# A fused attention and gated-MLP kernel: warm-up operands, weight loads, one input load and one logits group moved

## The chip, the core and the metric

One core of a Trainium2 chip runs the whole program: TensorE (PE, matmuls into PSUM), VectorE (DVE), ScalarE (ACT), GpSimd (POOL), and SyncE (SP), which here only issues DMAs. The metric is the device time of one execution in microseconds (us), the median of several runs. Inputs and output lie in DRAM. A profile of one execution gives the times of single instructions.

## The reference

Two branches read the same layer-normalised x (2048 rows of 640, bfloat16) and are added to x:

```python
x = A_x
xn = _layernorm(x, axis=-1)
return x + _A_ref(xn, A_wqkv, A_wo) + _B_ref(xn, B_w_gate, B_w_up, B_w_down)

def _A_ref(x, wqkv, wo):
    H = 32; Dh = D // H                    # 32 heads of 20
    W, dil = 8, 2                          # each row looks at itself and 7 rows before it, 2 apart
    qkv = ...                              # x @ wqkv, split into q, k, v per head
    idx = pos[:, None] - off[None, :]      # off = 0, 2, ... 14; idx < 0 is masked
    logits = jnp.einsum("bhsd,bhswd->bhsw", q, kg) * scale
    attn = _softmax(jnp.where(mask, logits, -1e9), axis=-1)
    o = jnp.einsum("bhsw,bhswd->bhsd", attn, vg)
    return (heads side by side) @ wo

def _B_ref(x, w_gate, w_up, w_down):       # F = 1536
    return ((x @ w_gate) * (x @ w_up)) @ w_down
```

## The kernel before

The 2048 rows are 16 tiles of 128 (t), four to a chunk (c = 0 to 3). Each tile of x is loaded, normalised and transposed into `xnT`, so that its 640 features lie in five slices of 128 partitions. The tiles 0 to 2 are transposed by PE (L385, with an ACT copy out of PSUM), the others by a DMA transpose that SP issues (L379). Normalisation is done on DVE for chunks 0 and 1 (statistics L253, one step `rstd` on POOL L267, application L272), and on ACT for chunks 2 and 3 (L326 and L330 the sums, L340 the application).

For each chunk PE makes q, k and v (`proj`, L500; single tiles of chunk 0 in `tile_part`, L464) and ACT copies them to bfloat16. Attention runs on DVE: `products` multiplies q by k at the eight offsets (`pw`, L555), `fold` adds parts of the head dimension (L530, the last step L535 writes `qk`); `logits` (L582) finishes these sums on PE with a 0/1 matrix `Ek` into the PSUM tile `pl`; `softmax` takes the maximum (L618), subtracts (L622), has ACT take the exponential (L632), sums (L640), inverts (L643) and scales into `a` (L649). `a` is stored to DRAM (`aD`, L658) and read back four times, spread over the 20 features of each head (`aE`, L666). `av` multiplies by v (L698) and adds over the eight offsets (L708, L706) into `oT`. GR says in how many groups the logits and softmax of a chunk are done: 1 for chunks 0 to 2, and 2 for chunk 3. With two groups, each has half of the rows; the tiles are half as wide, and the `av` products are two per tile.

The gated branch (`glu`, L746) makes gate and up for 12 blocks of 128 features; ACT copies them to `gs` and `us` (L751), DVE multiplies them into `hT` (L763). `down` adds hT times `wd` (L809) and oT times `wo` (L812) in the same PSUM tile, and the result goes out by ACT (L824) and an accumulating DMA from POOL (L853) onto a copy of x; the last two tiles add x on DVE (L820) and are stored by SP (L851).

The order of the work is not that of the source. Each piece is a `Step` with an engine, a duration that the author set, and what it depends on; `Plan.order` plays them out on these durations, and on each engine takes the ready step with the least slack (logits are urgent: they go as soon as they are ready by the plan). The instructions are then written in that order, and each engine runs its own in order. `PACE` stretches the planned durations of an engine: 1.03 for DVE before. PSUM tiles named `ps` rotate over six buffers.

At the start SP loads x of tiles 0 to 2. DVE sets `wz` (the tile `gs`, L214) to zero, then a corner of wq (`hold`, L206), for which the wq loads wait. ACT issues wq in three pieces (slice 0; 1 and 2; 3 and 4; L203), then x of tile 3. PE runs ten warm-up matmuls on `wz` (L244), and then the transposes and projections of tile 0, each part as soon as its piece of wq is there. SP goes on with wk, x of tiles 4 to 7, the transpose of tile 3, wv, and the transposes of tiles 4 to 7, then wg, x of tiles 9 to 12, wu, wd and wo. x of tile 8 is loaded by POOL, once the transpose of tile 3 has released its buffer.

Of the kernel before, what the change touches and what calls it, by code (L numbers as in the profile page):

```python
# [9 lines left out]
ACT = mybir.ActivationFunctionType  # L10
# [22 lines left out]
class Plan:  # L33
# [1 line left out]

    LAG = 0.06
    RAW = 0.116
    PACE = {"DVE": 1.03, "ACT": 1.0}
    INORDER = ("DVE", "PE", "ACT")

    def __init__(self):
# [2 lines left out]
    def add(self, eng, cost, fn, deps=(), occ=None, after=(), kb=0):  # L44
        k = self.PACE.get(eng, 1.0)
        s = Step(eng, cost * k, fn, deps, None if occ is None else occ * k, after)
        s.kb = kb
        s.pace = k
        s.idx = len(self.steps)
        self.steps.append(s)  # L50
        return s
# [60 lines left out]
def kernel(  # L112
# [11 lines left out]
    nc = tc.nc  # L124
    P = nc.NUM_PARTITIONS
    x_flat = A_x.flatten_outer_dims()
    out_flat = out.flatten_outer_dims()
    S, D = x_flat.shape
# [8 lines left out]
    KT = D // P  # L137
    FT = F // P
    NT = S // P
    CH = 4  # L140
    NCH = NT // CH
    CS = CH * P
    JL = P // H
    NS = D // 2
    BF, F32 = dt.bfloat16, dt.float32
# [10 lines left out]
    wv = const.tile([P, KT, D], BF, name="wv")  # L156
# [10 lines left out]
    add = plan.add  # L167
    T = {}

    def new(key, shape, dtype, tag, bufs, pool=None):  # L170
        t = (pool or sb).tile(shape, dtype, name=tag, tag=tag, bufs=bufs)
        T[key] = t
        return t


    def load_x(t, eng=None):
        def fn():
            x = new(("x", t), [P, D], BF, "x", 5)
            (eng or nc.sync).dma_start(out=x[:], in_=x_flat[t * P : (t + 1) * P, :])
        return fn  # L180

    X = {}

    def wload(dst, src, eng=None):
        return lambda: (eng or nc.sync).dma_start(out=dst[:], in_=src.rearrange("(i p) f -> p i f", p=P))
# [10 lines left out]
    def load(at, fn, deps=()):  # L196
        s = chain[0] = add("SP", 2.0, fn, deps, occ=0.45, after=[chain[0]])
        s.floor = at
        return s

    def part(r, lo, hi):
        src = A_wqkv[lo * P : hi * P, r * D : (r + 1) * D].rearrange("(i p) f -> p i f", p=P)
        return lambda: nc.scalar.dma_start(out=WT[r][:, lo:hi, :], in_=src)  # L203

    def hold(dst):
        return lambda: nc.vector.memset(dst[0:1, 0, 0:2], 0.0)  # L206
# [3 lines left out]
    X[2] = load(4.9, load_x(2))  # L210

    def consts0():
        wz = new("wz", [P, CS], BF, "gs", 5)
        nc.vector.memset(wz[:], 0.0)  # L214
        hold(wq)()
        nc.vector.memset(mhalf[:], -0.5)  # L216
        make_identity(nc, ident[:])
# [15 lines left out]

    C0 = add("POOL", 0.6, consts0)
    WP = []
    for lo, hi, at in ((0, 1, 4.4), (1, 3, 5.1), (3, KT, 5.5)):
        WP.append(add("ACT", at, part(0, lo, hi), [C0], occ=0.48, after=WP[-1:]))
    X[3] = add("ACT", 5.2, load_x(3, nc.scalar), occ=0.45, after=[WP[2]])
    TB = add("ACT", 1.6, table, after=[X[3]])

    def warm():
        ps = psum.tile([P, 512], F32, name="ps", tag="ps", bufs=6)
        for _ in range(10):
            nc.tensor.matmul(ps[:], lhsT=T["wz"][:, 0:P], rhs=T["wz"][:], start=True, stop=True)  # L244

    main = add("PE", 4.4, warm, [C0])


    def ln_stats(t, g):
# [30 lines left out]
    def behind(s, a):  # L280
        s.after.append(a)
        s.deps.append(a)
        plan.steps.remove(s)
        plan.steps.append(s)
# [5 lines left out]
    def st_in(t, g, d=None):  # L290
        return inline("DVE", 0.48, ln_stats(t, g), [d or X[t]], 0.395)
# [64 lines left out]
    def pe_main(cost, fn, deps=(), banks=1):  # L356
        nonlocal main
        waits = []
        for k in range(banks):
            if len(ring) + k >= 6:  # L360
                waits.append(ring[len(ring) + k - 6])
        main = add("PE", cost + 0.165, fn, [main, *waits, *deps], occ=cost)
        return main
# [6 lines left out]
    def transposes(t):  # L370
        c, q = divmod(t, CH)

        def slot():
            if q == 0:
                new(("xnT", c), [P, KT, CS], BF, "xnT", XB)

        def dma():
            slot()
            nc.sync.dma_start_transpose(out=T["xnT", c][:, :, q * P : (q + 1) * P], in_=T["x", t][:])  # L379

        def piece(g0, g1, n):
            def pe():
                ps = new(("pst", t, n), [P, KT, P], BF, "ps", 6, psum)
                for g in range(g0, g1):
                    nc.tensor.transpose(ps[:, g, :], T["x", t][:, g * P : (g + 1) * P], ident[:])  # L385

            def ev():
                if n == 0:
                    slot()
                nc.scalar.copy(T["xnT", c][:, g0:g1, q * P : (q + 1) * P], T["pst", t, n][:, g0:g1, :])  # L390
            return pe, ev

        if t in PIECES:
            for n, (g0, g1) in enumerate(PIECES[t]):
                p, e = piece(g0, g1, n)
                w = g1 - g0
                a = pe_main(w * 0.056, p, [XT.get((t, n), XT[t])])
                a = add("ACT", 0.16 + w * P / 1200, e, [a, TT.get(t)], occ=0.07 + w * P / 1200)
                TT[t] = a
                TX.setdefault(t, []).append((g0, g1, a))  # L400
                ring.append(a)
            if t:
                behind(PV[t - 1][0], TT[t])
        else:
            if c < 2:
                a = TT[t] = chain[0] = add("SP", 3.0, dma, [XT[t]], occ=1.28, after=[chain[0]])
            else:
                a = TT[t] = add("SP", 2.8, dma, [XT[t], GP.get(c - XB)], occ=1.28, kb=200)
        if t + 5 < W:
            X[t + 5] = load((11.0, 11.5, 14.2)[t], load_x(t + 5), [a])  # L410
        elif t == 3 or 8 <= t < NT - 5:
            X[t + 5] = add("POOL", 6.0, load_x(t + 5, nc.gpsimd), [a], occ=0.45, kb=160)

    LL = {}
    GR = (1, 1, 1, 2)
    PV = {}
    R = {}
    PROJ = ("q", "k", "v")
# [12 lines left out]
    def halo(c, r):  # L431
# [10 lines left out]
        else:  # L442
            w = LL.get((c - 2, GR[c - 2] - 1)) if r == 1 else O16.get(CH * (c - 1) - 1)
            HALOCP[r, c] = add("ACT", 0.25, fn, [w, *R[r, c - 1]])

    def lhs(r, i, j):
        return WT[r][:, i, :].rearrange("p (c b) -> p c b", b=KT)[:, :, j]
# [7 lines left out]
    def tile_part(r, t, n, g0, g1, deps):  # L455
        c, q = divmod(t, CH)
        j0, j1 = JS[n]

        def pe():
            if g0 == 0:  # L460
                new(("psv", r, t, n), [P, 512], F32, "ps", 6, psum)
            for j in range(j0, j1):
                for i in range(g0, g1):
                    nc.tensor.matmul(T["psv", r, t, n][:, (j - j0) * P : (j - j0 + 1) * P], lhsT=lhs(r, i, j),  # L464
                                     rhs=T["xnT", c][:, i, q * P : (q + 1) * P], start=(i == 0 and j == j0), stop=(i == KT - 1),
                                     skip_group_check=True)

        ws = WQ[: (1, 2, 2, 3, 3)[g1 - 1]] if r == 0 else WW[r]
        return pe_main((g1 - g0) * (j1 - j0) * 0.056, pe, [*deps, *ws], banks=1 if g0 == 0 else 0)

    def tile_evict(r, t, n, a):
# [21 lines left out]
    def proj(c, r, lo=0, n=CS):  # L493
        for j in range(KT):
# [11 lines left out]
            ts = range(c * CH + lo // P, c * CH + (lo + n) // P)  # L506
            old = LL.get((c - 2, GR[c - 2] - 1)) if r < 2 else O16.get(CH * (c - 1) - 1)
            a = pe_main(KT * (n / 2400 + 0.0027), pe, [*WW[r], *[TT[t] for t in ts], old])
# [55 lines left out]
    before = {}  # L564
    order = [(c, g) for c in range(NCH) for g in range(GR[c])]
    for a, b in zip(order, order[1:]):
        before[b] = a

    def logits(c, g):
        n = (c, g)  # L570
        E = CS // 4 // GR[c]

        def lg():
            if g == 0:
                new(("lps", c), [P, 2 * CS], F32, "pl", 1, psum)
            l = T["lps", c][:, g * W * E : (g + 1) * W * E].rearrange("p (w s) -> p w s", w=W)
            sets = 3 - GR[c]
            for b in range(sets):
# [5 lines left out]

        took = 0.2 + 0.2195 * 2 / GR[c]
        folds = [FO[4 * c + u] for u in range(4) if GR[c] == 1 or u // 2 == g]
# [282 lines left out]
    WQ = WP  # L869
# [10 lines left out]
    for k, (g0, g1, x) in enumerate(TX[0]):  # L880
        for n in range(2):
            if k == 2 and n == 1:
                a = st_in(2, 0, None)
                a = st_in(2, 1, a)
                apply_in(1)
                transposes(1)
                WV = None
            a0[n] = tile_part(0, 0, n, g0, g1, [x])
            if k == 2:
                tile_evict(0, 0, n, a0[n])  # L890
# [8 lines left out]
    proj_tile(0, 2, (0,))  # L899
    apply_in(3)  # L900
    transposes(3)
    WV = load(14.6, wload(wv, A_wqkv[:, 2 * D : 3 * D]))
    WW = (WP, [WK], [WV])
    proj_tile(0, 2, (1,))
    proj(0, 1, 0, 3 * P)
# [5 lines left out]
        ln(t)  # L911
        transposes(t)
    WL["g"] = load(28.5, wload(wg, B_w_gate))
    for t in range(9, 13):
        X[t] = load(30.0, load_x(t), [TT[t - 5]])
    WL["u"] = load(36.0, wload(wu, B_w_up))
    proj(0, 2)
# [68 lines left out]
```

## Time and profile before

| | |
|---|---|
| median of 3 runs | 257.65 us (257.4 to 259.34) |
| profiled execution | 258.23 us, its span 256.5 us |
| instructions in the profile | 3786 |
| PE busy | 251.8 us, 98% of the span |
| DVE busy | 223.5 us, 87% |
| ACT busy | 129.1 us, 50% |
| POOL busy | 41.8 us, 16% |
| DMA | 24.65 MB, 96 GB/s over the span |
| chain that ended last | PE 96%, DMA 2% |

The span runs from the first instruction to the last; the time of an execution holds some more around it. A busy PE is counted from a matmul's start to its modelled end, and matmuls overlap, so what a group of them costs is read from the distance between starts, as the chain does: there a piece "151.02 0.55 PE pl L582 x8" starts at 151.02 us and holds the chain for 0.55 us, for eight matmuls. In a timeline a line has start, duration, engine, line of the kernel, operation, the tile written and read, the count, and in brackets how long the engine stood idle before and what ended that. PEld are weight loads, ACTq, SPq and POOLq the issuing of DMAs.

### The profile page before, as it was taken

The numbers are of one execution on the slowest core, as the hardware profiler recorded it, in microseconds if no ns is written. First come the engines' busy times: TensorE is split into PE (matmuls) and PEld (weight loads), VectorE is DVE, ScalarE is ACT, GpSimd is POOL, SyncE is SP. The second block draws the span as 40 slices with busy tenths as digits, with TensorE's granted clock in tenths as the row PEclk, the third lists the DMA queues.
The fourth block names the chain that finished last, engine by engine and source line by source line (L and its number), as shares of the span: only waits on it lengthen the run. The fifth ranks groups of instructions, "written<-read, shape, count | busy, mean of one in ns | idle before, by whom it ended". The sixth has DMA issues, their size and how long they took to land.

```text
span 256.5 us, 3786 instructions
## 1 busy us (share of the span) xinstructions
PE 251.8 (98%) x1481; PEld 141.4 (55%) x1481; DVE 223.5 (87%) x273; ACT 129.1 (50%) x250; POOL 41.8 (16%) x61
## 2 busy tenths in 40 slices
PE   7999999999999999999999999999999999999995
PEld 2885554444456775444455766444457754445763
DVE  5769999997999999999999999799999999994011
ACT  2656689786589164655554114545542135554100
POOL 2432000411100711004100112000293120000110
PEclk9999999999999999999999999999999999999999
DMA  6895999058500278051400132520005534000221
GB/s 216 259 192 105 399 391 335 3 152 179 157 0 3 27 95 85 7 191 44 170 0 0 17 38 27 145 88 0 0 3 127 130 31 102 23 0 3 24 27 51
DMA packets 21953, 24.65 MB, mean 96 GB/s; under 512 B 10032, under 2 KB 18352, under 8 KB 21872
## 3 DMA queue, kind: packets, MB, share of 16 engines
q1 hardware_dynamic: 18672, 17.86, 24.0%
q0 software_dynamic: 2432, 5.57, 13.5%
q10 hardware_dynamic: 832, 0.98, 1.2%
q8 instruction: 11, 0.18, 0.3%
q14 instruction: 6, 0.05, 0.1%
HBM read 18.61 MB, written 5.96 MB: 96 GB/s over the span
## 4 chain that ended last, share of the span: by engine, by line
PE 96%; DMA 2%; ACTq 0%; DVE 0%; issue 0%
PE ps L746 40%; PE ps L500 23%; PE ps L809 20%; PE ps L812 8%; PE ps L464 3%; DMA wq<-in_A_wqkv_dram 2%; PE pl L582 1%; ACTq L203 0%; PE ps L385 0%; DVE x L820 0%; DVE gs L214 0%; DVE mhalf L216 0%; DVE dm L189 0%
## 5 line engine op out<-in xcount | busy, mean ns | idle before, releaser
L746 PE MATMUL ps<-xnT,wg 128*128 128x512 bf16 x240 | 59.7, 379 | 0.0
L746 PE MATMUL ps<-xnT,wu 128*128 128x512 bf16 x240 | 59.6, 379 | 0.0
L809 PE MATMUL ps<-wd,hT 128*128 128x320 bf16 (+2 forms) x384 | 57.4, 299 | 0.0
L698 DVE TENSOR_TENSOR av<-v,aE 128x5120 bf16<-128x5120 bf16 (+1 forms) x20 | 45.6, 2286 | 3.7 <-DMA aE<-aD 3.7
L809 PEld LDWEIGHTS <-hT 128*128 128x128 bf16 x384 | 37.0, 98 | 16.3 <-issue 0.7
L555 DVE TENSOR_TENSOR pw<-qk 128x2560 bf16<-128x2560 bf16 x28 | 40.8, 1485 | 0.1
L746 PEld LDWEIGHTS <-wu 128*128 128x128 bf16 x240 | 23.5, 98 | 28.3
L746 PEld LDWEIGHTS <-wg 128*128 128x128 bf16 x240 | 23.3, 98 | 28.1 <-issue 0.5
L751 ACT CAST us<-ps 128x512 bf16<-128x512 f32 x48 | 28.1, 585 | 21.2 <-PE ps L746 20.2
L751 ACT CAST gs<-ps 128x512 bf16<-128x512 f32 x48 | 28.1, 585 | 20.4 <-PE ps L746 20.3
L708 DVE TENSOR_TENSOR av<-av 128x2560 bf16<-128x2560 bf16 (+1 forms) x32 | 36.9, 1153 | 0.2
L824 ACT COPY y<-ps 128x320 f32<-128x320 f32 x28 | 11.5, 426 | 42.6 <-PE ps L812 32.7
L853 POOL DMA_DIRECT2D out_dram<-y x14 | 12.2, 871 | 105.3 <-ACT y L824 86.7
L812 PE MATMUL ps<-wo,oT 128*128 128x320 bf16 (+2 forms) x160 | 27.0, 299 | 0.0
L504 ACT CAST qk<-ps 128x512 bf16<-128x512 f32 (+1 forms) x35 | 19.9, 569 | 12.2 <-PE ps L500 12.2
L530 DVE TENSOR_TENSOR pw<-pw 128x2048 bf16<-128x2048 bf16 (+1 forms) x28 | 25.6, 951 | 0.0
L500 PE MATMUL ps<-xnT,wv 128*128 128x512 bf16 x100 | 22.3, 379 | 0.0
L763 DVE TENSOR_TENSOR hT<-gs,us 128x512 bf16<-128x512 bf16 x48 | 19.7, 417 | 2.5 <-ACT us L751 2.3
L500 PE MATMUL ps<-xnT,wk 128*128 128x512 bf16 (+1 forms) x100 | 20.9, 366 | 0.0
L812 PEld LDWEIGHTS <-oT 128*128 128x128 bf16 x160 | 15.5, 98 | 6.3
L790 POOL COPY gate<-hT 1x1 bf16<-1x1 bf16 x4 | 10.6, 2652 | 51.2 <-DVE hT L763 51.2
L500 PEld LDWEIGHTS <-wv 128*128 128x128 bf16 x100 | 11.6, 118 | 9.7 <-issue 0.4
(67 smaller groups left out, 200.8 us busy)
## 6 DMA issues: line engine op xcount, KB each, us to landing
aE<-aD SPq DMA_DIRECT2D x12, 256.0 KB, 4.0
out_dram<-y POOLq DMA_DIRECT2D x14, 160.0 KB, 3.8
wg<-in_B_w_gate_dram SPq DMA_DIRECT2D x1, 1920.0 KB, 9.1
wu<-in_B_w_up_dram SPq DMA_DIRECT2D x1, 1920.0 KB, 13.0
wd<-in_B_w_down_dram SPq DMA_DIRECT2D x1, 1920.0 KB, 17.9
out_dram<-in_A_x_dram POOLq DMA_DIRECT2D x3, 640.0 KB, 4.2
x<-in_A_x_dram SPq DMA_DIRECT2D x11, 160.0 KB, 5.3
aE<-aD SPq DMA_DIRECT2D x8, 128.0 KB, 2.6
```

The lines of the kernel that those rows point to most:

```text
L500: nc.tensor.matmul(T[key][:, 0:n], lhsT=lhs(r, i, j), rhs=T["xnT", c][:, i, lo : lo + n], start=(i == 0), stop=(i == KT - 1))
L504: nc.scalar.copy(where(r, c, j, j + 1, lo, n)[:, 0, :], T[key][:, 0:n])
L530: nc.vector.tensor_tensor(w[:, :, lo:hi, :], w[:, :, lo:hi, :], w[:, :, a:b, :], ALU.add)
L555: nc.vector.tensor_tensor(o, qh, kh, ALU.mult)
L698: nc.vector.tensor_tensor(o, v, w, ALU.mult)
L708: nc.vector.tensor_tensor(v[:, 0:k], v[:, 0:k], v[:, k : 2 * k], ALU.add)
L746: nc.tensor.matmul(ps[:], lhsT=(wu if r else wg)[:, i, f * P : (f + 1) * P], rhs=T["xnT", c][:, i, :], start=(i == 0), stop=(i == KT - 1))
L751: nc.scalar.copy(s[:], T[key][:])
L763: nc.vector.tensor_tensor(h[:], T["gs", c, f][:], T["us", c, f][:], ALU.mult)
L809: nc.tensor.matmul(ps, lhsT=T["hT", c, f][:, q * P : (q + 1) * P], rhs=wd[:, f, sl], start=(f == 0), stop=(f == FT - 1 and not wo_part))
L812: nc.tensor.matmul(ps, lhsT=T["oT", t][:, g, :], rhs=wo[:, g, sl], start=False, stop=(g == KT - 1 and f1 == FT))
L853: nc.gpsimd.dma_start(out=out_flat[t * P : (t + 1) * P, :], in_=T["y", t][:], accum_op=ALU.add)
```

## The change

- The warm-up matmuls read a constant tile of ones that the framework sets before the kernel, instead of `wz`; `wz` and its memset are gone, the warm-up step depends on nothing, and there are eleven instead of ten.
- wq is loaded in two pieces (slices 0 to 2; 3 and 4). The matmuls of slices 0 to 2 wait for the first piece, the others for both.
- wv's load comes ahead of x of tile 7 and the transpose of tile 3 on SP.
- x of tile 8 is loaded by SP, behind wg and ahead of tile 9, and no longer by POOL.
- Chunk 3 has one group of logits and softmax like the others.
- The planner's pace for DVE is 1.02 instead of 1.03. It changes no instruction, but it may change their order.

In the order of the built program, PE's matmuls stand as before but for the logits of chunk 2, which come 17 matmuls earlier, and those of chunk 3: in place of four early in the gated branch of chunk 2 and four in its `down`, eight stand together in `down`, 34 matmuls ahead of where the second four were. On DVE some products, folds and hT multiplies change places by a few positions in each chunk.

```diff
--- before.py
+++ after.py
@@ -35,7 +35,7 @@
 
     LAG = 0.06
     RAW = 0.116
-    PACE = {"DVE": 1.03, "ACT": 1.0}
+    PACE = {"DVE": 1.02, "ACT": 1.0}
     INORDER = ("DVE", "PE", "ACT")
 
     def __init__(self):
@@ -210,8 +210,6 @@
     X[2] = load(4.9, load_x(2))
 
     def consts0():
-        wz = new("wz", [P, CS], BF, "gs", 5)
-        nc.vector.memset(wz[:], 0.0)
         hold(wq)()
         nc.vector.memset(mhalf[:], -0.5)
         make_identity(nc, ident[:])
@@ -233,17 +231,18 @@
 
     C0 = add("POOL", 0.6, consts0)
     WP = []
-    for lo, hi, at in ((0, 1, 4.4), (1, 3, 5.1), (3, KT, 5.5)):
+    for lo, hi, at in ((0, 3, 4.6), (3, KT, 5.6)):
         WP.append(add("ACT", at, part(0, lo, hi), [C0], occ=0.48, after=WP[-1:]))
-    X[3] = add("ACT", 5.2, load_x(3, nc.scalar), occ=0.45, after=[WP[2]])
+    X[3] = add("ACT", 5.0, load_x(3, nc.scalar), occ=0.45, after=[WP[1]])
     TB = add("ACT", 1.6, table, after=[X[3]])
 
     def warm():
         ps = psum.tile([P, 512], F32, name="ps", tag="ps", bufs=6)
-        for _ in range(10):
-            nc.tensor.matmul(ps[:], lhsT=T["wz"][:, 0:P], rhs=T["wz"][:], start=True, stop=True)
-
-    main = add("PE", 4.4, warm, [C0])
+        one = nc.const_aps.tensor(1.0, [P, CS], BF)
+        for _ in range(11):
+            nc.tensor.matmul(ps[:], lhsT=one[:, 0:P], rhs=one, start=True, stop=True)
+
+    main = add("PE", 4.7, warm)
 
 
     def ln_stats(t, g):
@@ -408,11 +407,11 @@
                 a = TT[t] = add("SP", 2.8, dma, [XT[t], GP.get(c - XB)], occ=1.28, kb=200)
         if t + 5 < W:
             X[t + 5] = load((11.0, 11.5, 14.2)[t], load_x(t + 5), [a])
-        elif t == 3 or 8 <= t < NT - 5:
+        elif 8 <= t < NT - 5:
             X[t + 5] = add("POOL", 6.0, load_x(t + 5, nc.gpsimd), [a], occ=0.45, kb=160)
 
     LL = {}
-    GR = (1, 1, 1, 2)
+    GR = (1, 1, 1, 1)
     PV = {}
     R = {}
     PROJ = ("q", "k", "v")
@@ -465,7 +464,7 @@
                                      rhs=T["xnT", c][:, i, q * P : (q + 1) * P], start=(i == 0 and j == j0), stop=(i == KT - 1),
                                      skip_group_check=True)
 
-        ws = WQ[: (1, 2, 2, 3, 3)[g1 - 1]] if r == 0 else WW[r]
+        ws = WQ[: 1 + (g1 > 3)] if r == 0 else WW[r]
         return pe_main((g1 - g0) * (j1 - j0) * 0.056, pe, [*deps, *ws], banks=1 if g0 == 0 else 0)
 
     def tile_evict(r, t, n, a):
@@ -884,7 +883,7 @@
                 a = st_in(2, 1, a)
                 apply_in(1)
                 transposes(1)
-                WV = None
+                WV = load(13.8, wload(wv, A_wqkv[:, 2 * D : 3 * D]))
             a0[n] = tile_part(0, 0, n, g0, g1, [x])
             if k == 2:
                 tile_evict(0, 0, n, a0[n])
@@ -899,7 +898,6 @@
     proj_tile(0, 2, (0,))
     apply_in(3)
     transposes(3)
-    WV = load(14.6, wload(wv, A_wqkv[:, 2 * D : 3 * D]))
     WW = (WP, [WK], [WV])
     proj_tile(0, 2, (1,))
     proj(0, 1, 0, 3 * P)
@@ -911,7 +909,7 @@
         ln(t)
         transposes(t)
     WL["g"] = load(28.5, wload(wg, B_w_gate))
-    for t in range(9, 13):
+    for t in range(8, 13):
         X[t] = load(30.0, load_x(t), [TT[t - 5]])
     WL["u"] = load(36.0, wload(wu, B_w_up))
     proj(0, 2)
```

## The prediction

> **What bounds the kernel now.** I read the page (busy shares), a table of windows, the chain of waits in order of time, and the timelines of the first 20 us and of DVE from 146 us on. First the page's line of busy time and, from the windows, the row of the long middle stretch (start:end, its length, PE busy, PEld, DVE, ACT, POOL, clock, DMA share, GB/s):
>
> ```profile
> PE 251.8 (98%) x1481; PEld 141.4 (55%) x1481; DVE 223.5 (87%) x273; ACT 129.1 (50%) x250; POOL 41.8 (16%) x61
> ```
>
> ```profile
> 8.03:253.63 245.60, 245.58 (x1451) 138.81 (x1451) 218.57 (x254) 126.72 (x245) 39.73 (x51) 1.00 0.38 93
> ```
>
> From 8.03 to 253.63 TensorE (PE) rests 0.02 us. So three things alone can move the time: when that dense stretch begins, how much PE work is in it, and whether an edit opens a hole in it. The order of PE's matmuls stays as it was, except for where the logits stand. The beginning, in the timeline and then in the chain (start, duration, what):
>
> ```profile
> 0.93 0.27 DVE L214 MEMSET gs<- 128x256 uint32 x1 [0.93 <-PEq L970]
> ...
> 1.26 1.40 ACTq L203 DMA_DIRECT2D wq<-in_A_wqkv_dram  x3
> ...
> 1.26 4.45 PE L244 MATMUL ps<-gs 128*128 128x512 bf16 x10 [1.26 <-DVE dm L189]
> ...
> 7.69 0.43 DVE L272 TENSOR_SCALAR x<-x,mv,rstd 128x640 bf16<-128x640 bf16 x1
> ```
>
> ```profile
> 2.17 5.82 DMA wq<-in_A_wqkv_dram
> ```
>
> The dense stretch waits for the third piece of wq, issued at 2.17 and landed at 7.99. Right behind that limit stands another: the transposes of tile 1 (the first at 8.40) need DVE's normalised x1, done at 7.69 + 0.43 = 8.12.
>
> **The change, part by part.** *Warm-up and wq.* The memset of `gs` (0.27 us) goes; the small memset of wq behind it, for which ACT's first wq load waits, moves from 1.15 to about 0.93, and ACT's issue from 1.26 to about 1.04. Three issues (1.40 us, 0.47 each) become two, so the last piece is issued at about 1.5 instead of 2.17. It lands 0.67 earlier if issue sets that, 0.22 if the transfers do. The DMA engines were 0.84 busy in the window 1.26 to 5.70, so I take the smaller: 7.75. PE then does its six matmuls of 8.03 (0.32 us) from 7.8 and reaches the transposes at 8.12 to 8.17, where x1 stops it; before, it began them at 8.40. Gain 0.25 us; 0.5 at most (if x2, for which DVE waits 0.33 at 6.89, also comes sooner), 0 at least, since an earlier wq shares the engines with x1, for which DVE already waits 0.22 at 4.62. The first piece now holds three slices instead of one, and PE wanted slice 0 at 6.43; but it stood until 7.20 for slices 1 and 2 anyway. The warm-up waits for nothing now: 11 matmuls of 0.427 (the weight loads of L244 start 0.43 apart) from about 0.85 end at 5.55 instead of 5.5, ahead of the first transpose at 5.80, so the eleventh is free.
>
> *x8 and wv.* Before, x8's load sat on POOL and held it. The timeline:
>
> ```profile
> 11.11 1.31 SPq L379 DMA_TRANSPOSE xnT<-x  x1
> 12.48 1.92 SPq L185 DMA_DIRECT2D wv<-in_A_wqkv_dram  x1
> ...
> 15.86 0.76 POOL L179 DMA_DIRECT2D x<-in_A_x_dram  x1 [2.39 <-DMA xnT<-x]
> ...
> 17.26 0.45 DVE L272 TENSOR_SCALAR x<-x,mv,rstd 128x640 bf16<-128x640 bf16 x1 [2.18 <-POOL rstd L267]
> ```
>
> Without it the rstd of tile 5 no longer queues behind POOL's wait, and DVE gets the 2.18 us back. PE did not wait for them (the dense row above covers it), so this is slack for tiles 5 to 7 and 0 us of time. On SP x8's load is one more issue (0.4 us) behind wg's; its data comes near 28 us, and its first reader, on ACT, ran at 31.6: 0.
> wv passes x7 and the transpose of tile 3 on SP. That transpose took 4.4 us from its issue to landing, so until 15.5; PE reads the tile at 16.27. Now 800 KB of wv are queued ahead of it, issued at about 9.3 behind x6 (issued 8.87). DMA ran at 380 GB/s until 11 and would go on so: wv 2.1 us, x7 0.4, then the transpose's own 160 KB, 0.8 to 1: 14.5, if nothing holds it. But DMA stood almost still from 13.0 to 14.5 (12 GB/s there) with the transpose and wv pending; if that hole recurs, 16.2. PE is there at 16.0. I take a wait of 0.2, bounds 0 and 1.5. Behind it on SP stand the transposes of tiles 4 to 7, whose reader comes at 24.4, eight microseconds later: 0.
>
> *Logits.* One group in chunk 3, as in the others. The chain:
>
> ```profile
> 151.02 0.55 PE pl L582 x8
> 151.56 1.74 PE ps L809 x12
> ...
> 166.15 0.33 PE pl L582 x4
> ...
> 206.49 0.33 PE pl L582 x4
> 206.82 1.74 PE ps L809 x12
> ```
>
> Twice 0.33 becomes once 0.55, and one step of 0.11 goes (1.74 against the usual 1.63 of L809 x12): 0.22 us of PE work less. But the order of instructions shows more. With its pace for DVE changed, the planner sets logits earlier on PE: chunk 2's by 17 matmuls of 0.136 (2.3 us, to 148.7), and the one group of chunk 3 stands 34 matmuls (4.6 us) ahead of the old second group, at 206.42 - 4.6 - 0.33 - 0.11 = 201.4. DVE must have its folds (L535) done by then, and all of PE is queued behind that wait. DVE's timeline:
>
> ```profile
> 146.20 1.29 DVE L535 TENSOR_TENSOR qk<-pw 128x1024 bf16<-128x1024 bf16 x2
> ...
> 167.03 2.83 DVE L698 TENSOR_TENSOR av<-v,aE 128x5120 bf16<-128x5120 bf16 x1 [2.07 <-DMA aE<-aD]
> ...
> 203.08 1.28 DVE L535 TENSOR_TENSOR qk<-pw 128x1024 bf16<-128x1024 bf16 x2
> ```
>
> Chunk 2: folds were done at 147.5, so the slack shrinks from 3.5 to 1.2 us. A product of 1.40 moved from chunk 1's filling to here, and DVE arrives 1.40 earlier for it: no wait. Chunk 3: from the last oT of chunk 2 (192.16) to the last fold (204.36) DVE needed 12.2 us. Softmax group 0 (0.72 + 0.61 + 0.72 + 0.59 + 0.60 = 3.24) leaves that stretch; a product (1.40) and one hT (0.34) enter, with small waits between: about 10.7. That oT itself comes 0.75 sooner: the softmax of chunk 2 now starts after two products instead of three (1.40), two more hT stand behind it (0.67). So the folds are done at 192.16 - 0.75 + 10.7 = 202.1 and PE waits 0.7; or not at all, if the wait of 2.07 for aE shrinks too. I take 0.5, bounds 0 and 1.0.
> Behind it DVE has one softmax and four `av` products of 2.73 instead of two and eight of 1.40. It starts later, at about 203, and takes 7 us to `a`; the trip from the `a` store over DRAM to aE takes 5 to 7; each tile then 6 (2.73 + 1.40 + 0.74 + 0.41 and two hT). The four oT are there at about 222, 228, 234 and 240; PE reads them from 236 on, 4.6 apart: 0.
>
> **Sum.** -0.25 (start) + 0.2 (tile 3) - 0.22 (logits) + 0.5 (folds of chunk 3) = +0.2 us. The profiled execution took 258.23 (its span of 256.5 and 1.7 around it), so it would take 258.4; the runs' median lies 0.6 below the profiled one, so I forecast 257.8.
>
> **The rivals.** *Tile 3 behind wv.* The hole in the DMA traffic recurs and the transpose lands at 17.5: PE waits 1.5 instead of 0.2, 259.1. For it speaks the 1.92 us that SP needed to issue wv with a transpose pending; against it that wv is now issued first.
> *DVE late from chunk 1 on (slower).* With a product less to do, DVE reaches chunk 1's first `av` at 114.19 - 1.40 = 112.8. aE lands at about 112.7 if the trip takes 5.0 us again (2.1 from store to aE issue, 2.9 to landing). Chunk 0's took 4.7 + 3.2 = 7.9. At 7.9 DVE stands for 2.8 us; PE, with 1.2 of slack at chunk 2's logits, then waits 1.6 there, 0.7 more than I took at chunk 3's, and 0.7 as later DVE work stays behind: +3.0, 260.8. It costs from a trip of 6.2 us on. Against it: DMA had nothing else to move around 108 to 113.
> *No wait opens.* Tile 3 in time, folds in time, the start gains 0.5: -0.7 - 0.2, 256.9.
> *The clock.* The warm-ups run at half rate: 0.427 for 512 columns, where L746 later takes 26.0 us for 120, 0.217 each. If full rate came only at 8 us, the 26 matmuls of 128 columns before it would take 0.05 more each, 1.3, of which PE's holes hide 0.5: +0.8, 258.6. The Trainium skill (TensorE: Matmul & The Clock Gate, Part 1) says that a free-running window of about 3.4 us decides, so that the moment differs from run to run. By that rule an earlier start of PE makes a late clock rarer.
>
> **Chances.** Forecast 0.50, no wait 0.17, tile 3 0.15, DVE late 0.13, clock 0.05. The range goes from just under the no-wait case to between tile 3 and DVE late: 256.7 to 260.0. A measurement of this kernel tells about 1% from no change. Over 1% faster (under 255.1) is none of the cases: 0.04 for what I overlook, taken from the first two. Over 1% slower (over 260.2) is the DVE case, 0.13. Within 1%: 0.83.
>
> **What would show it.** Right: the last wq landing near 7.7 and PE dense from 7.8; under 0.5 us of PE idle ahead of the tile 3 matmuls at 16; chunk 2's logits near 148.5 with no idle before, chunk 3's near 201 to 202 with up to 1 us, its end set by DVE's fold; last PE matmul between 253 and 254.5. Wrong: over 1 us of PE idle at one of these places, a wait of DVE for aE of over 1 us near 113, or a dense stretch that begins after 8.03.

## The result and the profile after

The changed kernel takes 259.55 us, the median of 9 runs (259.21 to 260.41); the kernel before took 257.65 in 9 runs beside it. The ratio is 1.0078, with a 95% interval of 1.0062 to 1.0095: slower by 0.8%, a small change, but its interval lies clear of 1. The forecast was 257.8. Five of the nine runs lie at 259.21 to 259.55, four at 260.14 to 260.41. The profiled execution is one of the four: 260.26, against 258.23 before, 2.03 us more. Three single executions of the kernels below took 267 us and more, and are left out of the medians here; as one of them is the only profiled execution of experiment 1, its trace is read for DMAs and for the start alone.

The page's busy line, then three windows that follow the kernel's stages: up to the first transpose, up to the matmuls of tile 3, and from there to the end (start:end, its length, PE, PEld, DVE, ACT, POOL, granted clock, DMA share, GB/s).

```profile
PE 252.2 (98%) x1482; PEld 142.7 (55%) x1482; DVE 223.4 (86%) x263; ACT 129.0 (50%) x249; POOL 41.3 (16%) x60
```

```profile
0.80:6.63 5.83, 3.93 (x12) 1.32 (x12) 2.56 (x12) 1.49 (x2) 1.27 (x5) 1.00 0.79 252
6.63:18.18 11.55, 11.22 (x115) 9.53 (x115) 8.69 (x31) 6.97 (x19) 4.45 (x17) 0.85 0.95 233
18.18:255.27 237.09, 237.06 (x1356) 131.80 (x1356) 211.82 (x221) 120.54 (x229) 35.40 (x34) 1.00 0.34 86
```

From 18.18 on PE is as dense as before (0.03 us of rest). The loss lies ahead of 18.18: PE stands for 1.85 us before its first transpose, and in the second window the mean clock is 0.85. The chain of waits and the timeline of that stretch after the change, and then four lines of the timeline before:

```profile
1.27 4.16 DMA x<-in_A_x_dram
5.43 0.02 issue
5.45 0.89 DVE st L252 x2
6.34 0.25 DVE x L271
...
6.82 4.85 DMA x<-in_A_x_dram
...
12.25 5.89 DMA xnT<-x
18.14 0.05 issue
18.18 2.99 PE ps L463 x50
```

```profile
0.85 3.92 PE L243 MATMUL ps<-const-bfloat16-1.0 128*128 128x512 bf16 x11 [0.85 <-PEq L968]
...
0.96 0.97 ACTq L203 DMA_DIRECT2D wq<-in_A_wqkv_dram  x2
...
5.45 0.89 DVE L252 BATCH_NORM_STATS2 st<-x 128x6 f32<-128x320 bf16 x2 [0.46 <-DMA x<-in_A_x_dram]
...
6.63 0.91 PE L384 MATMUL ps<-ident,x 128*128 128x128 bf16 x5 [1.85 <-DVE x L271]
...
7.33 2.45 PE L463 MATMUL ps<-xnT,wq 128*128 128x128 bf16 x21
...
9.57 0.74 PE L384 MATMUL ps<-ident,x 128*128 128x128 bf16 x5
...
18.18 1.48 PE L463 MATMUL ps<-xnT,wq 128*128 128x128 bf16 x23 [0.31 <-DMA xnT<-x]
```

```profile
4.62 0.89 DVE L253 BATCH_NORM_STATS2 st<-x 128x6 f32<-128x320 bf16 x2 [0.22 <-DMA x<-in_A_x_dram]
...
5.80 0.80 PE L385 MATMUL ps<-ident,x 128*128 128x128 bf16 x5
...
7.20 1.36 PE L464 MATMUL ps<-xnT,wq 128*128 128x128 bf16 x16 [0.33 <-DMA wq<-in_A_wqkv_dram]
...
16.27 1.56 PE L464 MATMUL ps<-xnT,wq 128*128 128x128 bf16 x25
```

Three things are to be seen. wq is no longer in the chain; x of tile 1 has taken its place. It landed at 5.43 instead of 4.59, and since the first transpose stands behind x1's statistics in DVE's order, that transpose began at 6.63 instead of 5.80: +0.83. Next, the 21 matmuls of 7.33 took 2.45 us, where the same 21 take 1.42 in experiment 5, and the five transposes of 9.57 took 0.74 instead of 0.45. The granted clock was full from 3.68 to 7.09, half from 7.09 to 10.51, and full again. From the start of the first transpose to the first matmul with wk (13.65) this makes 7.02 us instead of the 5.78 of experiment 5: 1.24 more. And the transpose of tile 3, issued at 12.25, landed at 18.14; PE had been ready 0.47 earlier. Against these stand 0.63 us of PE's pauses between 6.4 and 8.4 of before, while wq and x1 were late, which are gone (the same stretch took 6.41 there). 0.83 + 1.24 + 0.47 - 0.63 = 1.91: tile 3 begins at 18.18 instead of 16.27.

After that the changed kernel is quicker. Its last matmul starts at 255.03, 1.64 later than before (253.39), so 0.27 has come back. The chain at the logits, and DVE's timeline there:

```profile
150.57 0.55 PE pl L581 x8
151.11 1.74 PE ps L808 x12
...
203.30 0.55 PE pl L581 x8
203.84 1.74 PE ps L808 x12
```

```profile
201.57 1.29 DVE L534 TENSOR_TENSOR qk<-pw 128x1024 bf16<-128x1024 bf16 x2
203.90 1.22 DVE L617 TENSOR_REDUCE m<-pl 128x128 f32<-128x1024 f32 x1 [1.04 <-PE pl L581]
```

DVE's last fold was done at 202.86, 0.37 ahead of PE's first logits matmul (203.23). No wait opened at either logits group.

The missing 0.31 of the span lies behind the last matmul. The last store landed at 255.43 before and at 257.07 after; the span ended 1.04 us later before, and 1.35 after. The experiments show why.

### The profile page after: what moved, and what is told of

Same layout as the page of the kernel before. It is cut to its first block, busy times and chain, and to the rows that moved or that the text cites. A ratio compares the mean times of both kernels' runs of the same rounds, so it can differ in the third digit from the quotient of the medians.

```text
span 258.4 us, 3768 instructions
## 1 busy us (share of the span) xinstructions
PE 252.2 (98%) x1482; PEld 142.7 (55%) x1482; DVE 223.4 (86%) x263; ACT 129.0 (50%) x249; POOL 41.3 (16%) x60
## 3 DMA queue, kind: packets, MB, share of 16 engines
HBM read 18.61 MB, written 5.96 MB: 95 GB/s over the span
## 4 chain that ended last, share of the span: by engine, by line
PE 92%; DMA 6%; DVE 1%; SPq 0%; issue 0%
PE ps L745 40%; PE ps L499 21%; PE ps L808 20%; PE ps L811 8%; DMA x<-in_A_x_dram 3%; DMA xnT<-x 2%; PE ps L463 1%; PE pl L581 1%; DVE st L252 1%; SPq L179 0%; DVE x L819 0%; DVE x L271 0%; SPq L185 0%
## 5 line engine op out<-in xcount | busy, mean ns | idle before, releaser
L697 DVE TENSOR_TENSOR av<-v,aE 128x5120 bf16<-128x5120 bf16 x16 | 45.1, 2821 | 4.5 <-DMA aE<-aD 4.4
```

The lines of the kernel that those rows point to most:

```text
L697: nc.vector.tensor_tensor(o, v, w, ALU.mult)
```

## The experiments

The theory: the start lost twice. The first piece of wq (480 KB) is issued 0.3 us ahead of x1 and is served ahead of it (the order), and wv stands ahead of the transpose of tile 3 (the place of wv). One logits group gains, as it should. The rivals: the half clock, the two pieces as such, the folds of chunk 3. Times are medians; the kernel before had 257.75 to 257.76 in all three groups of runs.

**1. wq in three pieces again, all else as changed.**

```diff
-    for lo, hi, at in ((0, 3, 4.6), (3, KT, 5.6)):
+    for lo, hi, at in ((0, 1, 4.4), (1, 3, 5.1), (3, KT, 5.5)):
```

> The changed kernel with wq again in three pieces (slice 0; 1 and 2; 3 and 4), all else as changed. Order theory: transfers are served in the order in which SP and ACT issue them, so x1 (issued 1.27 us) lands late because 480 KB of wq were issued ahead of it at 0.96. With 160 KB ahead of it x1 lands near 4.4 us instead of 5.43, the first transpose comes near 5.7 instead of 6.63, and the median falls to 257.0 to 257.7. wv theory (the transpose of tile 3 is late because wv is ahead of it): x1 back in time, but the median stays above 258.5. Planner theory (logits and DVE's order): no change, 259.3.

258.56 (258.25 to 258.93), ratio 1.0029 (1.0017 to 1.0041). x1 landed at 4.11, and the first transpose, which waits for DVE, started at 5.69: that part came back as expected. The time came back by half only, which is the case of the wv theory.

**2. wq's issue moved behind that of x1 by two idle memsets (issue 1.63 instead of 0.96).**

```diff
+        wz = new("wz", [P, CS], BF, "gs", 5)
+        for _ in range(2):
+            nc.vector.memset(wz[:], 0.0)
         hold(wq)()
```

> The changed kernel with two memsets of 0.2 us each back on DVE ahead of the one that wq's first load waits for, so that this load is issued at about 1.45 us, behind x1 (1.27), still in two pieces. Order theory: x1 lands near 4.0 us, earlier than in the kernel before (4.59), and x0 at about 3.0; first transpose near 5.4; median 257.0 to 257.6. Rival, the load on the DMA engines: wq takes its share of them whenever it comes, x1 lands near 5 again and the median stays above 258.5.

258.64, ratio 1.0042 (1.0020 to 1.0064). x1 landed at 3.61, and the first transpose began at 5.47. But now PE waited for wq, 0.96 from start to start, and wv still stands ahead of tile 3, so the time missed the 257.0 to 257.6 expected. The delay was too long; experiment 12 is the better dose.

**3. wv again behind the transpose of tile 3.**

```diff
-                WV = load(13.8, wload(wv, A_wqkv[:, 2 * D : 3 * D]))
+                WV = None
...
     transposes(3)
+    WV = load(14.6, wload(wv, A_wqkv[:, 2 * D : 3 * D]))
```

> The changed kernel with wv issued again behind the transpose of tile 3. wv theory: PE's wait before tile 3 at 18 us was made by wv, and nearly all of the 2 us come back: 257.4 to 257.8. Order theory: the start is as late as before this edit (first transpose at 6.6), only the wait of some 0.5 us at tile 3 can go: 258.6 to 259.2.

258.58, ratio 1.0045 (1.0025 to 1.0065): 0.97 less than the changed kernel. The transpose landed 3.7 us after its issue instead of 5.9, and PE went on at 16.55 with no pause, though the start was as late as before this edit (first transpose 6.72):

```profile
16.55 1.56 PE L463 MATMUL ps<-xnT,wq 128*128 128x128 bf16 x25
```

Three of its 11 runs still took 259.82 to 260.68, at a mean clock of 0.993 instead of 1.0.

**4. Two logits groups in chunk 3 again, and the pace of 1.03.**

```diff
-    PACE = {"DVE": 1.02, "ACT": 1.0}
+    PACE = {"DVE": 1.03, "ACT": 1.0}
...
-    GR = (1, 1, 1, 1)
+    GR = (1, 1, 1, 2)
```

> The changed kernel with two logits groups in chunk 3 and the planner's DVE pace 1.03 again. Theory that the one group gains 0.2 to 0.3 us as worked out: 259.5 to 259.9 median. Rival, that the new order of logits and DVE work costs the time: 257.4 to 258.

259.31, ratio 1.0056 (1.0037 to 1.0075), from five runs, two of them at a mean clock of 0.993: not told apart from 259.55. Its trace gave something else: the span ended 1.04 after the last landing, as before the change, and not 1.35 as in experiments 2 and 3. So the tail belongs to the number of groups, or to something that this number sets.

**5. Both undone: wq in three pieces and wv behind.** The diffs of 1 and 3.

> The changed kernel with both undone: wq again in three pieces, and wv again behind the transpose of tile 3. Theory (the loss at the start has two parts that add: 480 KB of wq ahead of x1, and wv ahead of the transpose of tile 3): x1 lands at 4.1 to 4.4, the first transpose starts at 5.7, the transpose of tile 3 is issued at 10.5 and lands by 15.0, PE has no gap before tile 3; last matmul at 253.1 to 253.4, the rest of the span 3.4 after it as in the other kernels with one logits group (3.1 with two), time 257.3 to 257.8. Rival (the loss is in what is left of the change: the constant as warm-up operand, one logits group, x8 on SP): 258.3 to 258.8, as with either undone alone.

257.78, ratio 1.0006 (0.9989 to 1.0023), its runs 257.64 to 259.05. The two losses are separate and together are the whole: 257.78 + 0.80 (experiment 3 over this one) + 0.78 (experiment 1 over this one) = 259.36, against 259.28 for the median of the changed kernel's five lower runs. The chain, PE from the first transpose on:

```profile
5.67 0.24 DVE x L271
...
6.22 0.54 PE ps L384 x4
6.76 1.26 PE ps L463 x21
...
11.91 4.06 PE ps L499 x25
15.97 2.79 PE ps L463 x50
```

Nothing but PE stands between 5.96 and the matmuls of tile 3.

**6. The kernel before with two pieces of wq, nothing else.**

```diff
-    for lo, hi, at in ((0, 1, 4.4), (1, 3, 5.1), (3, KT, 5.5)):
+    for lo, hi, at in ((0, 3, 4.6), (3, KT, 5.6)):
```

> The kernel before, with wq in two pieces and nothing else changed; wq is issued at 1.26, at the same time as x1 (1.27). Theory (transfers are served in the order of issue): 480 KB beside x1; x1 lands at 5.0 to 5.4 instead of 4.59, first transpose 0.4 to 0.8 later, time 258.0 to 258.5. Rival (it was the earlier issue, not the size, that held x1 back): x1 lands by 4.7, the last piece of wq earlier than 7.99, time 257.3 to 257.7.

257.45, ratio 0.9982 (0.9967 to 0.9997): the rival held. x1 landed at 4.13, although a piece of 480 KB was issued beside it. Two pieces alone gain some 0.3 us. (The plan also sets chunk 0's logits five matmuls earlier on PE; PE waits nowhere in this trace.) So the size alone is not the fault; the lead of 0.3 us has to come into it. Of the versions whose median settled, this is the fastest, and the one whose interval lies below 1.

**7. The kernel before with one logits group and the pace of 1.02.** The diff of 4, reversed.

> The kernel before, with one logits group in chunk 3 and the pace of 1.02. Theory (logits cost 0.25 less on PE, and no wait opens at 148 or 202; but five DMAs fewer shift the last store's semaphore to an early place in the list that SP walks through at the end, at 0.06 a step): last matmul 0.25 earlier against its start, the span's end 3.4 after it instead of 3.1, time 257.5 to 257.8, no difference. Rival (the prediction's: DVE's folds come late in chunk 3): a PE gap of 0.5 to 1.0 before the logits at 201 to 203, 258.0 to 258.4. Second rival (only the logits count): 257.3 to 257.45.

257.63, ratio 0.9994 (0.9972 to 1.0016): no difference, as expected. The span ended 1.35 after the last landing, so the tail eats what the logits gain.

**8. The changed kernel with 16 warm-ups.**

```diff
-        for _ in range(11):
+        for _ in range(16):
...
-    main = add("PE", 4.7, warm)
+    main = add("PE", 6.8, warm)
```

> The changed kernel with 16 warm-up matmuls instead of 11, so that PE is busy until about 6 us. Theory (the clock falls back to half in some runs because PE is idle for 2 us between the warm-up and the first transpose): no profile or run with a mean clock of 0.993, full rate from about 4 us without a break, times 259.1 to 259.6 and none above 259.9 but for strays, median 259.3. Rival (the fallback does not depend on PE's idle time): a third to a half of the runs again at 0.993 and 260.0 to 260.5. If the added matmuls delay the first transpose (they end after 6.6): the same times plus the delay.

259.31 (258.99 to 259.64, 11 runs), ratio 1.0057 (1.0041 to 1.0072). No run is in the upper cluster any more. The longer planned step also sets the logits of chunks 0 and 1 earlier on PE, by 5 and 17 matmuls; PE waits 0.05 us there at most. The same stretch of both traces, first the changed kernel, then with 16 warm-ups:

```profile
7.09:10.51 3.42, 3.42 (x34) 3.37 (x33) 3.09 (x12) 1.40 (x6) 1.26 (x3) 0.50 0.81 249
```

```profile
7.09:10.51 3.42, 3.42 (x56) 3.23 (x55) 3.10 (x13) 2.23 (x9) 1.25 (x3) 1.00 0.85 253
```

34 matmuls at clock 0.50, 56 at 1.00. This removes the upper cluster, some 1.0 us where it falls (260.33 against 259.28, the medians of the two clusters), and leaves the 1.5 us of the other runs. Three of the four upper runs of the changed kernel show a mean clock of 0.993; the fourth (260.4) shows 1.0, so the clock does not account for it.

**9. The kernel before with two pieces and one logits group.** The diffs of 6 and 7. With the count of DMAs that SP and ACT issue, the place of the last store's semaphore in SP's final list changes: 62 before, 57 after the change, 56 here.

> The kernel before with two parts of the change: wq in two pieces, and one logits group in chunk 3 with the pace of 1.02. It loads and stores by SP and ACT with 56 DMAs instead of 62. Theory (the completion semaphores of these DMAs rotate over eight, and the last store's now is the eighth in the list that SP walks through at the end): the span ends 0.9 to 1.0 after the last store has landed (before: 1.04), the logits gain 0.25 and the two pieces 0.3, time 257.1 to 257.25, the fastest of all. Rival (the tail belongs to one logits group, whatever the number of DMAs): the span ends 1.3 to 1.4 after the landing, time 257.4 to 257.6. Second rival (the gain of two pieces was an accident): 257.4 to 257.6 with a tail of 0.9 to 1.0.

Half a miss, and the most telling run. The end went as expected: 0.92 from the last landing to the end of the span. Five runs took 257.08 to 257.62, three of them the lowest of the whole study; the other seven took 259.05 to 259.90. Over all twelve the median is 259.25, the ratio 1.0025 (0.9995 to 1.0055). The profiled one is of the seven (259.90). PE's timeline at the logits of chunk 3, and DVE's at chunk 2's first `av`:

```profile
202.03 0.39 PE L582 MATMUL pl<-qk,Ek 128*32 128x512 bf16 x2
202.92 0.40 PE L582 MATMUL pl<-qk,Ek 128*32 128x512 bf16 x4 [0.50 <-DVE qk L535]
203.52 0.39 PE L582 MATMUL pl<-qk,Ek 128*32 128x512 bf16 x2 [0.20 <-DVE qk L535]
```

```profile
167.79 2.83 DVE L698 TENSOR_TENSOR av<-v,aE 128x5120 bf16<-128x5120 bf16 x1 [2.43 <-DMA aE<-aD]
```

This is the wait for folds that the prediction had put at 0.5, and more: 1.27 us at the logits of chunk 3 (1.82 from their first matmul to the next group at 203.85, against 0.55 in experiment 10), another 0.59 at hT around 191 to 194, and 0.33 at chunk 2's logits at 148.4. DVE was behind early on, by 2.98 us at the first softmax, and then chunk 2's trip of `a` over DRAM held it for 2.43.

**10. The same with x of tile 8 on SP.**

```diff
-        elif t == 3 or 8 <= t < NT - 5:
+        elif 8 <= t < NT - 5:
...
-    for t in range(9, 13):
+    for t in range(8, 13):
```

> The same with x of tile 8 on SP, as in the change: 57 DMAs on SP and ACT. Theory: the last store's semaphore is the first in the list, and the span ends 1.3 to 1.4 after the landing: 0.35 to 0.4 slower than the run without it, 257.45 to 257.65; POOL no longer holds rstd of tile 5, which is worth nothing. Rival (x8 on POOL costs time): 257.1 or less. Second rival (the place in the list costs nothing): the same time as without it within 0.1.

257.64, ratio 0.9989 (0.9974 to 1.0003), lowest 257.45. The tail was 1.34, and the lowest runs are 0.37 above those of 9: the expected price of the place in the list. But x8 is worth more than nothing: no run compared took over 258.52, where seven of twelve did without it, and PE's and DVE's instructions stand in the same order in both. The logits of chunk 3:

```profile
200.46 0.62 PE L582 MATMUL pl<-qk,Ek 128*32 128x512 bf16 x8
```

All eight went in one go. With x8 on SP, DVE reached the first softmax 1.6 us behind PE's logits (39.91 to 41.52); with it on POOL 3.0 (40.44 to 43.42). How this shortens chunk 2's trip is not shown. Nor does x8 on POOL always cost this much: in experiment 7, which has it there too, DVE was 2.5 behind at the first softmax, the folds of chunk 2 came 0.04 ahead of PE, PE waited at no logits, and one of twelve runs took over 258.5 (259.93).

**11. The kernel before with wv ahead of the transpose of tile 3.** The diff of 3, reversed.

> The kernel before with wv ahead of x of tile 7 and the transpose of tile 3 on SP, and nothing else changed. Theory (800 KB ahead of the transpose delay it): the transpose of tile 3 lands at 16.3 to 17.5 instead of 14.3 to 15.5, PE waits 0.5 to 1.2 for it, time 258.2 to 258.9. Rival (in the changed kernel the transpose was late only because the start was): a wait under 0.3, 257.6 to 257.95.

259.26, ratio 1.0054 (1.0033 to 1.0075), more than expected. Its chain:

```profile
10.45 5.73 DMA xnT<-x
16.18 0.05 issue
16.23 0.81 PE ps L464 x11
```

With x1 in time the transpose still takes 5.73 from its issue, against 4.44 before. PE waited 0.63 there from start to start, and 0.61 at 24.2 for ACT's copy of v. The profiled execution took 258.85, so the trace explains 1.2 of the 1.5 us of the median.

**12. The changed kernel with only the old memset back ahead of wq's hold; nothing reads it.**

```diff
+        wz = new("wz", [P, CS], BF, "gs", 5)
+        nc.vector.memset(wz[:], 0.0)
         hold(wq)()
```

> The changed kernel with the memset of wz back ahead of the hold of wq, read by nothing (0.27 us of DVE): wq's first piece is issued at 1.26 instead of 0.96, beside x1 and not 0.3 ahead of it; the size of the piece stays 480 KB. Theory (the lead of 0.3 us holds x1 back, not the size of the piece alone): x1 lands at 4.1 to 4.6 instead of 5.4, the first transpose starts at 5.5 to 5.8; PE still waits 0.4 to 0.9 for tile 3; the last store's semaphore is second or first as in the changed kernel; time 257.9 to 258.5. Rival (480 KB are too much wherever they stand): x1 at 5.0 or later, 258.9 to 259.5.

258.36, ratio 1.0019 (1.0006 to 1.0033): 1.2 us faster than the changed kernel, and 0.9 faster than its five lower runs, by 0.27 us of added DVE work. x1 landed at 4.21, the first transpose began at 5.52. The DMA queues from 3.0 to 4.2 us (q1 is SP's with x, q10 ACT's with wq; packets, MB, share of the engines), first the changed kernel, then this:

```profile
q10 hardware_dynamic: 303, 0.38, 89.4%
q1 hardware_dynamic: 37, 0.04, 8.9%
```

```profile
q10 hardware_dynamic: 174, 0.22, 53.6%
q1 hardware_dynamic: 96, 0.10, 29.7%
```

With wq issued at 0.96, x1 gets 37 packets through in that stretch; with wq at 1.24 (x1 at 1.26 to 1.27 in both) 96. This shows the order theory in a corrected form. The size alone does not hold x1 back (experiments 6 and 12), and neither does the lead alone: in experiments 1 and 5 the first piece leads by the same 0.3 us, but has 160 KB, and x1 landed at 4.11 and 4.37. It takes a large piece with a lead.

**The end of the span.** In its last steps SP goes through a list of semaphores in a fixed order, about 0.06 us a step. The completions of the DMAs of SP and ACT rotate over eight of them, so their number decides which one the last store has. In the trace of before SP passes that step at 255.44, and two more of the list follow; after the change it passes it at 257.08, and seven follow. The traces:

| kernel | DMAs of SP and ACT | place of the last store's semaphore | last landing to end, us |
|---|---|---|---|
| experiment 9 | 56 | 8 | 0.92 |
| before; 4; 11 | 62 | 6 | 1.04 |
| 6 | 61 | 5 | 1.10 |
| 1; 5 | 58 | 2 | 1.28 |
| after; 2, 3, 7, 8, 10, 12 | 57 | 1 | 1.34 or 1.35 |

One step of the list is 0.06 in each row. The waits that stand behind the last store's are paid after it has landed; those ahead of it are done while it is on its way. Two logits groups mean five more DMAs (one `aD`, four `aE`).

## Why the prediction was right or wrong

The range (256.7 to 260.0) and the likeliest sign (within 1%) held, but the median lies 1.75 above the forecast, and the range held only because it reached to the rivals: luck, as far as the mechanism goes. Of the four terms of the sum only that of the logits came out. By the prediction's own signs it was wrong: the dense stretch begins at 18.18 and not at 7.8, and the last matmul at 255.03 and not between 253 and 254.5.

*The start: failed.* "0 at least, since an earlier wq shares the engines with x1, for which DVE already waits 0.22 at 4.62" named the right collision and then put a floor of 0 under it. The term of -0.25 measured about +0.8: experiment 3 has the new start without the early wv and takes 258.58, against 257.76 for the kernel before. (The lead of the large piece costs 0.9, by 259.28 against the 258.36 of experiment 12; the two pieces give 0.3 back in experiment 6.) The working looked at the last piece of wq, which did land earlier (some 6.9 instead of 7.99) and was of no use; it did not ask what a first piece three times the size, issued 0.3 us ahead of x1, does to x1. The chain's row for wq shown of before (2.17, 5.82) also was a single execution's: in experiment 7, whose start is that of before, the last piece landed by 7.3 and PE did not wait for it. The 0.25 was partly in the median already.

The Trainium skill (DMA: Bandwidth & Descriptors, "Queues, rings and completion order") says that each DMA engine takes turns between the queues that have work for it, packet by packet. The rows of the changed kernel do not show such turns between SP's and ACT's queue: 303 packets to 37. Whether x1's packets were not yet in their queue or were passed over, these runs do not tell.

*Tile 3 behind wv: mis-sized.* The term of 0.2 measured 1.0 by the medians in the changed kernel (experiment 3; 0.7 between the runs with a mean clock near 1.0) and 1.5 in the kernel before (experiment 11, where the trace has 0.63 of it at tile 3 and 0.61 at ACT's copy of v). The rival "tile 3 behind wv" at 259.1 was the likelier case, and its condition, the hole in the DMA traffic, did recur. It only moved: after the change the engines moved 253 GB/s from 12 to 14 us, but 54 from 16.0 to 17.5, when wv had landed (15.99) and the transpose had not (18.14). The rows of the changed kernel, and then of experiment 11, where wv landed at 14.09 (the last figure is GB/s):

```profile
12.00:14.00 2.00, 2.00 (x35) 1.91 (x33) 1.93 (x7) 1.77 (x6) 0.80 (x8) 1.00 0.99 253
16.00:17.50 1.50, 1.50 (x11) 1.09 (x10) 0.00 (x0) 0.88 (x2) 0.54 (x1) 1.00 0.39 54
```

```profile
14.00:15.50 1.50, 1.50 (x11) 1.04 (x9) 0.56 (x2) 0.96 (x2) 0.00 (x0) 1.00 0.76 43
```

In experiment 5, with wv behind the transpose, 52 GB/s moved from 13.0 to 14.5, before the transpose landed at 14.51. So in these traces the hole goes with the transpose, and wv ahead of it adds its own transfer. No run separates the two.

*Logits: right.* 0.22 forecast, 0.27 in the traces; but the tail of 0.31 takes it back, a cost that the prediction did not know, and one group is worth 0 (experiment 7).

*Folds of chunk 3: did not open here.* The 0.5 measured 0 in the changed kernel, with 0.37 us to spare. The mechanism exists (experiment 9). What kept it shut in experiment 10 is x8 on SP, which the prediction had costed at nothing: right for PE there and then, but it can be cover for an edit 180 us later. That it is what kept the wait shut in the changed kernel is likely, not shown: that kernel was not run with x8 on POOL, and experiment 7 stayed shut without it. The rival "DVE late from chunk 1 on" is close to what experiment 9 shows, with the trip of chunk 2 in the place of chunk 1's.

*The clock: the reverse.* The forecast held that an earlier start of PE makes a late clock rarer. Full rate did come sooner (3.68 against 5.77), but the warm-up then also ended sooner, at 4.77 and not at the 5.55 worked out for half rate, and met a first transpose that came later. PE idled 1.85 of the 3.41 us to 7.09, and the next 3.41 ran at half rate. The Trainium skill (TensorE: Matmul & The Clock Gate, "Why this matters for your kernels") allows pauses up to about 3 us before the clock falls back; here half rate followed on a pause of 1.85, in the profiled run, while the 1.45 of experiment 3's profiled run was followed by full rate. In experiment 8, which closes most of the pause, no run shows a fall. Mean clocks of 0.991 to 0.993 came up in 3 of 9 runs of the changed kernel, 2 of 12 in experiment 2, 3 of 11 in 3, 2 of 5 in 4 and 1 of 9 in 11, and in none of the others. That the pause is the cause rests on experiment 8; how long a pause it takes is not measured beyond these two traces.

*What stays open.* Why the median of experiment 11 lies 0.4 above its profiled execution, and what sends the trip of chunk 2 into its long form. Over the profiles it goes with the order of two stores: where `aD` was issued 0.6 to 0.7 us behind an output store of POOL (before, 4, 6, 9, 11), 3.7 to 4.0 us passed until the issue of `aE`; where it was issued at another time, 2.1 to 3.1. Chunk 0's trip goes the same way: 4.5 to 5.2 us where `aD` was issued 0.96 behind POOL's copy of x into the output, 2.1 in experiments 1 and 5, where none had been issued yet. No run tested this. The pace of 1.02 was not run apart from the one group. Two pieces, one group and x8 on SP with a late place for the last semaphore was not run as one kernel.

## What to carry to other kernels

Here a large load issued 0.3 us earlier pushed back a small one that the next step waited for; before costing such an edit at "0 at least", ask which small, urgent transfer it now overtakes. An edit that is worth nothing in its own place may be the slack that another part of the same change lives on, so try parts alone and in pairs. And where a few tenths of a microsecond matter, count what the program does after its last store.

## What was not expected of the hardware

- A lead of 0.3 us of a 480 KB load on another queue delayed a 160 KB load by 1.2 us (5.43 against 4.21); a lead of 0.3 us of a 160 KB load did not (4.11 and 4.37).
- PE's clock fell back to half for 3.41 us after an idle stretch of 1.85 us, right behind a warm-up that had reached full rate.
- While a 160 KB DMA transpose was under way, the engines moved 12 to 54 GB/s for 1.5 us, wherever it stood (before, after, experiments 5 and 11).
- The order in which the completion semaphores are waited for at the end costs 0.06 us a step, 0.43 between the best and the worst place.
